# Reordering the first 18 microseconds of a mixer kernel: pair 8 before pair 6, tile 0 in halves, tile 3 through a DMA transpose

## The chip, the cores and the metric

The kernel runs on one core of one Trainium2 chip. The metric is the device time of one execution in microseconds. The time before the change is 136.75 us, the median of three runs (136.24, 136.75 and 136.87).

## The reference

The input x has 2048 rows of 512 values in bf16. A first layer normalizes each row, multiplies by w1 (512 x 512) and applies GELU. The result is shifted along the rows (one group of 128 columns by one row forward, one by one row back, one by two forward, one by two back), multiplied by w2 and added to x. A second layer normalizes that, multiplies by w3 (512 x 1792), applies GELU, multiplies by w4 (1792 x 512) and adds.

```python
def reference(x, w1, w2, w3, w4):
    B, S, D = x.shape
    h = _gelu(_layernorm(x, axis=-1) @ w1)
    c = D // 4
    g0 = jnp.pad(h[:, :, 0*c:1*c], ((0, 0), (1, 0), (0, 0)))[:, :S, :]
    g1 = jnp.pad(h[:, :, 1*c:2*c], ((0, 0), (0, 1), (0, 0)))[:, 1:, :]
    g2 = jnp.pad(h[:, :, 2*c:3*c], ((0, 0), (2, 0), (0, 0)))[:, :S, :]
    g3 = jnp.pad(h[:, :, 3*c:   ], ((0, 0), (0, 2), (0, 0)))[:, 2:, :]
    hs = jnp.concatenate([g0, g1, g2, g3], axis=-1) @ w2
    x1 = x + hs
    h2 = _gelu(_layernorm(x1, axis=-1) @ w3) @ w4
    return x1 + h2
```

## The kernel before

The 2048 rows are 16 tiles of 128 rows. Tile t holds the rows whose number modulo 16 is t, so a shift by one row is, for most tiles, the neighbouring tile.

The program is a list of named operations, each with what it reads and writes. `emit` turns these into semaphore waits. On each engine the operations run in order; the lists in `firsts` give that order by name for the start of the program, and what is not listed follows in the order of its `add`. An operation that waits holds up everything behind it on its engine. SyncE ("sp") is the queue from which nearly all DMAs are issued, so a DMA that waits for data holds up the DMAs listed behind it.

The first layer treats the tiles in two ways.

- Tiles 0 to 5 are "raw". The tile x is transposed as it was loaded: `tp` on TensorE (line 323) with `ev`, the copy out of PSUM on ScalarE (line 332), for tiles 0 to 3; `tdx`, a DMA transpose straight from memory (line 351), for tiles 4 and 5. `m1r` (line 378) multiplies it by w1 in four steps of 512 columns, `rc` (line 388) copies the result out, `zr` on VectorE (line 393) subtracts the mean times w1's column sums, and `g1r` (line 399) applies the scale and GELU. The column sums come from `cs0`, `cs1`, `cs2` and `cs` on TensorE (line 366), and `cse` copies them out (line 370). `th` is a DMA transpose of the result.
- Tiles 6 to 15 are normalized first: `st` and `ag` (statistics and aggregation on VectorE, lines 289 and 294), `rs` (the root, on GpSimd, for a pair of tiles, line 300), `nm` (the normalization on VectorE, line 309). A pair of them is then transposed, either by `tp` and `ev` (pairs 8 and 10) or by `td0`, a DMA transpose (line 343; pairs 6, 12 and 14). `m1p` multiplies a pair by w1 (line 410, 16 matmuls of 256 columns), and `g1p` or `g1s` applies GELU (lines 420 and 425).

`m2` (lines 436 and 450) multiplies by w2; a name with a, b or nothing at its end is a part of one tile's product. `x1` (line 460) adds x. The second layer repeats the statistics for x1 (`st1`, `ag1`, `rs1`, `nm1`) and transposes pairs by `td1` (line 343). `m3h` (line 492) multiplies the first four tiles, 8 to 11, by w3 in two halves: first the pair 8, which `td1_8` brings, then the pair 10 (`td1_10`). `m3` (line 468) and `m4` (line 511) do the rest, and `fin` and `out` add and store.

Loads: `ldx` for x (line 272), `ldw1` (line 542), `ldw2` (line 546), `ldw3a` (line 551, the first 1024 columns of w3, in four chunks), `ldw3b` (line 556), `ldw4`. Two of w1's chunks and x1 are loaded from ScalarE's queue. `wu` (line 534) is a run of matmuls on constants ahead of the first data.

PSUM has 8 banks. Raw tiles' transposes use banks 6 and 7, products of raw tiles banks 0 to 3, the column sums bank 4, the warm-up bank 5; the pair products use banks 2-3, 4-5, 0-1, 2-3 and 6-7.

Of the kernel before, what the change touches and what calls it, by code (L numbers as in the profile page):

```python
# [5 lines left out]
P = 128  # L6
ACT_F = mybir.ActivationFunctionType
ALU = mybir.AluOpType
BF16 = mybir.dt.bfloat16
# [17 lines left out]
class Program:  # L27
# [7 lines left out]
    def add(self, eng, name, fn, reads=(), writes=(), dma=False):  # L35
        self.ops.append(Op(name, eng, fn, reads, writes, dma))
# [135 lines left out]
def bass_standalone__mixer_s_mlp__prompt_kernel(nc: bass.Bass, x, w1, w2, w3, w4, out):  # L172
# [4 lines left out]
    DC = D // P  # L177
# [5 lines left out]
    xd = x[0].rearrange("(p t) d -> p t d", t=NT)  # L183
# [4 lines left out]
    with ExitStack() as es:  # L188
        sb = lambda name, shape, dt: es.enter_context(nc.sbuf_tensor(name, shape, dt))
        x_sb = sb("x_sb", [P, NT, D], BF16)  # L190
# [3 lines left out]
        xnT = sb("xnT", [P, NT, DC, P], BF16)  # L194
# [8 lines left out]
        w2_sb = sb("w2_sb", [P, DC, D], BF16)  # L203
        w3_sb = sb("w3_sb", [P, DC, F], BF16)
        w4_sb = sb("w4_sb", [P, FC, D], BF16)
        ident = sb("ident", [P, P], BF16)
# [3 lines left out]
        neghalf = sb("neghalf", [P, 4], F32)  # L210
        warm = sb("warm", [P, 1], F32)
        o_sb = sb("o_sb", [P, 4, D], BF16)
        ps = es.enter_context(nc.psum_tensor("ps", [P, 8 * 512], F32))
        psb = ps[:, :].bitcast(BF16)
        ones = nc.const_aps.tensor(1.0, [P, P], BF16)
        ones_wide = nc.const_aps.tensor(1.0, [P, 512], BF16)
        one_f = nc.const_aps.tensor(1.0, [P, 1], F32)

        hT = hTf[:, 16 : 16 + NT * DC * HW].rearrange("p (t j w) -> p t j w", t=NT, j=DC)
# [22 lines left out]
        W1 = [(("w1", c), 0) for c in range(DC)]  # L242
        W2 = [(("w2", c), 0) for c in range(DC)]
        pr = Program()
        add = pr.add

        def bank(b, n=1):
            return ps[:, 512 * b : 512 * (b + n)]

        def bres(b, n, tag):  # L250
            return [(("ps", b + i), tag) for i in range(n)]
# [19 lines left out]
        def load_x(t, n, eng="sp"):  # L271
            add(eng, f"ldx{t}", lambda e: e.dma_start(x_sb[:, t : t + n, :], xd[:, t : t + n, :]),  # L272
                writes=[(("x", i), 0) for i in range(t, t + n)], dma=True)
# [9 lines left out]
        def dst_of(layer, t):  # L283
            return (xn, t, ("xn", t), 0) if layer == 0 else (x1n, POS[t] % 8, ("x1n", POS[t] % 8), t)
# [29 lines left out]
        def tp(t, n, b, raw):  # L314
            src = x_sb if raw else xn
            rd = [(("x", i), 0) if raw else (("xn", i), 0) for i in range(t, t + n)]

            def f(e):
                ins = None
                for i in range(n):  # L320
                    for c in range(DC):
                        o = 1024 * b + (i * DC + c) * P
                        ins = e.transpose(psb[:, o : o + P], src[:, t + i, P * c : P * (c + 1)], ident[:])  # L323
                return ins

            add("pe", f"tp{t}", f, reads=rd + [("ident", 1)], writes=bres(b, 1, f"tp{t}"))

        def ev(t, n, b, eng="act"):
            src = psb[:, 1024 * b : 1024 * b + n * D]
            dst = xnT[:, t : t + n, :, :].rearrange("p t c s -> p (t c s)")  # L330
            if eng == "act":
                f = lambda e: e.activation(dst, src, ACT_F.Copy)  # L332
            else:
                f = lambda e: e.tensor_copy(dst, src)
            add(eng, f"ev{t}", f, reads=bres(b, 1, f"tp{t}"), writes=[(("xT", i), 0) for i in range(t, t + n)])


        def tdma(layer, t, n):
            dst = xnT if layer == 0 else x1nT
            src, k = dst_of(layer, t)[:2]  # L340
            p0 = t if layer == 0 else POS[t]
            add("sp", f"td{layer}_{t}",
                lambda e: e.dma_start(dst[:, p0 : p0 + n, :, :].rearrange("p t c s -> p (t c) s"),
                                      src[:, k : k + n, :].rearrange("p t d -> p (t d)"), transpose=True),
                reads=[dst_of(layer, i)[2:] for i in range(t, t + n)],
                writes=[(("xT", i) if layer == 0 else ("x1T", i), 0) for i in range(t, t + n)], dma=True)


        def tdma_x(t):
            add("sp", f"tdx_{t}",  # L350
                lambda e: e.dma_start(xnT[:, t : t + 2, :, :].rearrange("p t c s -> p (t c) s"),  # L351
                                      xd[:, t : t + 2, :].rearrange("p t d -> p (t d)"), transpose=True),
                writes=[(("xT", i), 0) for i in (t, t + 1)], dma=True)

        def tdma_h(t, n):
            add("sp", f"th_{t}",
# [17 lines left out]
        def m1r(t, b, c0=0, c1=DC):  # L374
            def f(e):
                ins = None
                for c in range(c0, c1):
                    ins = e.matmul(bank(b), xnT[:, t, c, :], w1_sb[:, c, :], start=(c == 0), stop=(c == DC - 1))  # L378
                return ins

            rd = [(("xT", t), 0)] + W1[c0:c1]
            if c0:
                rd += bres(b, 1, f"m1r{t}{c0}")
            end = f"{c1}" if c1 < DC else ""
            add("pe", f"m1r{t}{end}", f, reads=rd, writes=bres(b, 1, f"m1r{t}{end}"))

        def rc(t, b):
            add("act", f"rc{t}", lambda e: e.activation(yraw[:, t, :], bank(b), ACT_F.Copy),
                reads=bres(b, 1, f"m1r{t}"), writes=[(("yraw", t), 0)])
# [140 lines left out]
        def warmup(name, n, b):  # L530
            def f(e):
                ins = None
                for _ in range(n):
                    ins = e.matmul(bank(b), ones, ones_wide, start=True, stop=True)
                return ins

            add("pe", name, f, writes=bres(b, 1, name))
# [5 lines left out]
                writes=[(("w1", c), 0)], dma=True)  # L543

        def load_w2(c):
            add("sp", f"ldw2{c}", lambda e: e.dma_start(w2_sb[:, c, :], w2[P * c : P * (c + 1), :]),
                writes=[(("w2", c), 0)], dma=True)

        def load_w3a(c):
            add("sp", f"ldw3a{c}",  # L550
# [11 lines left out]
        load_w1(2, "act")  # L562
        load_w1(3, "sp")
        load_x(1, 1, "act")
        for t, n in ((6, 1), (7, 1), (2, 1), (8, 1), (3, 1), (9, 1), (10, 1), (11, 1), (12, 1), (13, 1), (14, 2), (4, 2)):
            load_x(t, n)
        for c in range(DC):
            load_w2(c)
        for c in range(DC):
            load_w3a(c)  # L570
        load_w3b()

        warmup("wu", 7, 5)
        YB = (0, 1, 2, 3, 0, 1)
        for c in range(DC):
            colsum(4, c)
        colsum_out(4)
        for t in range(R):
            if t < 4:
                tp(t, 1, 6 + t % 2, True)  # L580
                ev(t, 1, 6 + t % 2, "act")
            elif t == 4:
                tdma_x(t)
            cuts = [0, 1, 2, 3, 4] if t == 0 else [0, 2, 4] if t == 1 else [0, 4]
            for c0, c1 in zip(cuts, cuts[1:]):
                m1r(t, YB[t], c0, c1)
            rc(t, YB[t])
# [7 lines left out]
        for t in range(R, NT, 2):  # L595
# [2 lines left out]
                ev(t, 2, 6 + t // 2 % 2)  # L598
            else:
                tdma(0, t, 2)  # L600
        for t, b in ((6, 2), (8, 4), (10, 0), (12, 2), (14, 6)):
            m1p(t, b)
            if t == 10:
                g1s(t, b, 0)
                g1s(t, b, 1)
            else:
                g1p(t, b)
# [19 lines left out]
        for t in (8, 10):  # L627
# [7 lines left out]
            tdma(1, t, 2)  # L635

        firsts = {}
        firsts["pe"] = """wu tp0 cs0 cs1 m1r01 m1r02 tp1 m1r03 cs2 m1r0 cs tp2 m1r12 m1r1 tp3 m1r2 m1r3 m1r4 m1r5 tp8 m1p6
            tp10 m1p8 m1p10 m2_8a m2_9a m2_8 m2_9b m2_9 m2_10a m2_11a m2_12a m2_13a m1p12 m1p14 m2_10 m2_11
            m2_12b m2_13b m2_14a m2_15a m2_12 m2_13 m2_14b m2_15b m2_14 m2_15""".split()  # L640
        firsts["act"] = """ldw10 ldw12 ldx1 table ev0 ev1 rc0 ev2 ev3 rc1 rc2 rc3 rc4 rc5 ev8 cse g1p6 ev10 g1p8 g1s10 g1s11
            g1r0 g1r1 g1p12 g1p14 g2h_0_0_0 g2h_0_0_4 g1r2 g1r3 g2h_0_0_8 g2h_0_0_12 g1r4 g1r5""".split()
        firsts["dve"] = """pada padb padc padd pade padf st0_0 st0_6 st0_7 ag0_6 ag0_7
            st0_8 nm0_6 nm0_7 st0_9 ag0_8 ag0_9 st0_10 st0_11 nm0_8 nm0_9 ag0_10 ag0_11
            st0_12 nm0_10 nm0_11 st0_13 ag0_12 ag0_13 st0_14 st0_15 ag0_14 ag0_15 nm0_12 nm0_13 st0_1 ag0_0 ag0_1
            nm0_14 nm0_15 zr0 zr1 x1_8 x1_9 st1_8 st1_9 ag1_8 ag1_9 st0_2 nm1_8 nm1_9 st0_3 ag0_2 ag0_3 x1_10 x1_11 st1_10
            st1_11 ag1_10 ag1_11 x1_12 nm1_10 nm1_11 x1_13 x1_14 x1_15 zr2 zr3 st0_4 st0_5 ag0_4 ag0_5 zr4 zr5
            st1_12 st1_13 ag1_12 ag1_13""".split()
        firsts["pool"] = """ident0 ident1 neghalf stz ste rs0_6 rs0_8 rs0_10
            rs0_12 rs0_14 rs0_0 rs1_8 rs0_2 rs1_10""".split()  # L650
        firsts["sp"] = """ldx0 ldw11 ldx6 ldw13 ldx7 ldx2 ldx8 ldx3 ldx9 tdx_4 ldx10 ldx11 ldx12 td0_6 ldx13 ldx14 ldw20 ldw21 ldw22 ldw23 td0_12 td0_14 ldw3a0 ldw3a1
            ldw3a2 ldw3a3 th_0 td1_8 ldw3b ldx4 td1_10 th_2 th_4 td1_12 td1_14 ldw4""".split()

        slots = [4, 0, 2]
# [25 lines left out]
        def nm2(t):  # L680
            def f():
                norm(1, t)
                norm(1, t + 1)
                tdma(1, t, 2)

            return f
# [23 lines left out]
        for i, t in enumerate((0, 1, 2, 3, 4, 5, 6, 7)):  # L710
            b = (6, 7, 1)[i % 3]
# [11 lines left out]
        for q in (2, 3):  # L723
            for i in range(4):
                b = 6 + i % 2
# [40 lines left out]
```

## Time and profile before

| | |
|---|---|
| median of three runs | 136.75 us (136.24 to 136.87) |
| the profiled execution | 136.32 us |
| its span, first to last instruction | 134.5 us |
| TensorE busy | 130.8 us, 719 matmul records |
| VectorE busy | 58.3 us |
| ScalarE busy | 46.8 us |
| GpSimd busy | 12.5 us |
| DMA | 12.96 MB in 24376 packets |

The profiled execution is 1.8 us longer than its span; that part lies around the instructions. All times in the text below are counted from the start of the span. In the timeline and the chain the first number of a line is the start and the second the length. A matmul's record is longer than the distance to the next one, since matmuls are pipelined; the distances between starts tell how fast they go. Some matmul records are missing from the trace.

In the table of stretches, each engine has its busy time and, in brackets, its instructions; the last three numbers are the granted TensorE clock, the mean busy share of the DMA engines, and GB/s.

### The profile page before, as it was taken

The numbers are of one execution on the slowest core, as the hardware profiler recorded it, in microseconds if no ns is written. First come the engines' busy times: TensorE is split into PE (matmuls) and PEld (weight loads), VectorE is DVE, ScalarE is ACT, GpSimd is POOL, SyncE is SP. The second block draws the span as 40 slices with busy tenths as digits, with TensorE's granted clock in tenths as the row PEclk, the third lists the DMA queues.
The fourth block names the chain that finished last, engine by engine and source line by source line (L and its number), as shares of the span: only waits on it lengthen the run. The fifth ranks groups of instructions, "written<-read, shape, count | busy, mean of one in ns | idle before, by whom it ended". The sixth has DMA issues, their size and how long they took to land.

```text
span 134.5 us, 1794 instructions
## 1 busy us (share of the span) xinstructions
PE 130.8 (97%) x719; PEld 69.6 (52%) x729; DVE 58.3 (43%) x135; ACT 46.8 (35%) x56; POOL 12.5 (9%) x25
## 2 busy tenths in 40 slices
PE   7999999999999999999999999999999999999993
PEld 2446857678884444444444444444444444444452
DVE  0689999799967777762222000122200002322222
ACT  3488871507962036550001555200066630000000
POOL 2042422220330012220000000000000000000000
PEclk9999999999999999999999999999999999999999
DMA  4999379984465984444121000011110001111121
GB/s 123 317 247 217 115 145 246 255 292 83 78 128 100 295 262 78 78 80 78 39 68 49 5 0 0 0 39 39 41 37 5 0 0 39 39 39 39 44 75 42
DMA packets 24376, 12.96 MB, mean 96 GB/s; under 512 B 16688, under 2 KB 23600, under 8 KB 24368
## 3 DMA queue, kind: packets, MB, share of 16 engines
q1 hardware_dynamic: 23792, 12.42, 36.5%
q10 hardware_dynamic: 576, 0.43, 1.0%
q8 instruction: 6, 0.10, 0.3%
q14 instruction: 2, 0.02, 0.1%
HBM read 6.82 MB, written 2.10 MB: 66 GB/s over the span
## 4 chain that ended last, share of the span: by engine, by line
PE 89%; SPq 4%; DMA 2%; DVE 2%; issue 1%
PE ps L511 36%; PE ps L468 27%; PE ps L492 9%; PE ps L410 7%; PE ps L436 5%; PE ps L450 5%; DMA x_sb<-in_x_dram 2%; SPq L272 2%; SPq L351 1%; DVE st L289 1%; PE ps L323 1%; SPq L542 1%; DVE xn L309 0%; DVE o_sb L523 0%
## 5 line engine op out<-in xcount | busy, mean ns | idle before, releaser
L511 PE MATMUL ps<-w_sb,h2T 128*128 128x512 bf16 (+2 forms) x232 | 48.1, 366 | 0.3
L523 DVE TENSOR_TENSOR o_sb<-ps,x_sb 128x512 bf16<-128x512 f32 (+2 forms) x17 | 11.2, 660 | 61.2 <-PE ps L511 61.2
L479 ACT ACTIVATE h2T<-ps 128x1024 bf16<-128x1024 f32 x21 | 21.5, 1023 | 46.2 <-PE ps L468 46.2
L468 PE MATMUL ps<-x1nT,w_sb 128*128 128x512 bf16 x168 | 36.7, 379 | 0.0
L511 PEld LDWEIGHTS ps<-w_sb,h2T 128*128 128x128 bf16 x238 | 22.8, 98 | 25.9
L468 PEld LDWEIGHTS ps<-x1nT,w_sb 128*128 128x128 bf16 x168 | 16.4, 98 | 19.8
L289 DVE BATCH_NORM_STATS2 st<-x_sb 128x6 f32<-128x512 bf16 x32 | 20.9, 682 | 4.1 <-DMA x_sb<-in_x_dram 4.0
L300 POOL TENSOR_TENSOR rstd<-mv,neghalf 128x2 f32<-128x2 f32 x16 | 11.6, 725 | 46.1 <-DVE mv L294 46.1
L492 PE MATMUL ps<-x1nT,w_sb 128*128 128x256 bf16 x112 | 12.4, 273 | 0.0
L492 PEld LDWEIGHTS ps<-x1nT,w_sb 128*128 128x128 bf16 x112 | 11.0, 98 | 1.5
L460 DVE TENSOR_TENSOR x_sb<-ps,x_sb 128x512 bf16<-128x512 f32 x16 | 10.6, 685 | 2.5 <-PE ps L436 1.5
L410 PE MATMUL ps<-xnT,w_sb 128*128 128x256 bf16 x80 | 9.2, 273 | 0.0
L503 ACT ACTIVATE h2T<-ps 128x1024 bf16<-128x1024 f32 (+1 forms) x8 | 7.1, 913 | 6.0 <-PE ps L492 6.0
L410 PEld LDWEIGHTS ps<-xnT,w_sb 128*128 128x128 bf16 x80 | 7.6, 98 | 1.2
L309 DVE TENSOR_SCALAR x1n<-x_sb,mv,rstd 128x512 bf16<-128x512 bf16 x16 | 5.9, 409 | 5.3 <-POOL rstd L300 5.3
L450 PE MATMUL ps<-w_sb,hTf 128*128 128x512 bf16 x30 | 7.0, 379 | 0.1
L436 PE MATMUL ps<-w_sb,hTf 128*128 128x512 bf16 x31 | 6.9, 379 | 0.1
L378 PE MATMUL ps<-w_sb,xnT 128*128 128x512 bf16 x23 | 6.0, 382 | 0.1
L420 ACT ACTIVATE hTf<-ps 128x1024 bf16<-128x1024 f32 x4 | 4.1, 1023 | 4.2 <-PE ps L410 4.2
L332 ACT ACTIVATE xnT<-ps 128x512 bf16<-128x512 bf16 (+1 forms) x6 | 4.4, 738 | 2.3 <-PE ps L323 2.2
L436 PEld LDWEIGHTS ps<-w_sb,hTf 128*128 128x128 bf16 x32 | 3.1, 98 | 3.6
L294 DVE BATCH_NORM_AGGREGATE mv<-st 128x2 f32<-128x9 f32 x32 | 5.0, 185 | 0.0
(28 smaller groups left out, 36.8 us busy)
## 6 DMA issues: line engine op xcount, KB each, us to landing
out_dram<-o_sb SPq DMA_DIRECT2D x15, 128.0 KB, 1.8
w_sb<-in_w_dram SPq DMA_DIRECT2D x1, 1792.0 KB, 7.7
x_sb<-in_x_dram SPq DMA_DIRECT2D x11, 128.0 KB, 3.3
w_sb<-in_w_dram SPq DMA_DIRECT2D x4, 256.0 KB, 4.2
w_sb<-in_w_dram SPq DMA_DIRECT2D x6, 128.0 KB, 3.5
w_sb<-in_w_dram SPq DMA_DIRECT2D x1, 768.0 KB, 4.8
x_sb<-in_x_dram SPq DMA_DIRECT2D x2, 256.0 KB, 4.4
w_sb<-in_w_dram ACTq DMA_DIRECT2D x2, 128.0 KB, 3.2
```

The costliest lines, as they stand in the source:

```text
L289: add("dve", f"st{layer}_{t}", lambda e: e.bn_stats(st9[:, i, 0:6], src[:, t, :]), reads=[(r, 0)], writes=[(("st6", i), 0)])
L300: lambda e: e.tensor_tensor(rstd[:, i : i + n], mv[:, i : i + n, 1], neghalf[:, 0:n], ALU.pow),
L410: ins = e.matmul(dst, w1_sb[:, c, P * fc : P * (fc + 1)], xnT[:, t : t + 2, c, :], start=(c == 0), stop=(c == DC - 1))
L436: ins = e.matmul(bank(b), hTf[:, c0 : c0 + P], w2_sb[:, j, :], start=(j == 0), stop=(j == DC - 1))
L450: ins = e.matmul(bank(b), hTf[:, w[0] : w[0] + P], w2_sb[:, j, :], start=first and n == 0, stop=last and n == len(js) - 1)
L460: lambda e: e.tensor_tensor(x1_sb[:, t, :], bank(b), x_sb[:, t, :], ALU.add),
L468: ins = e.matmul(bank(b), w3_sb[:, c, P * fc : P * (fc + 1)], x1nT[:, 4 * q : 4 * q + 4, c, :], start=(c == 0), stop=(c == DC - 1))
L479: lambda e: e.activation(h2T[:, fc : fc + 2, q % 2, :], src, ACT_F.Gelu_apprx_tanh),
L492: ins = e.matmul(dst, w3_sb[:, c, P * (fc + i) : P * (fc + i + 1)], x1nT[:, t : t + 2, c, :], start=(c == 0), stop=(c == DC - 1))
L503: lambda e: e.activation(h2T[:, fc : fc + n, q % 2, 256 * k : 256 * (k + 1)], src, ACT_F.Gelu_apprx_tanh),
L511: ins = e.matmul(ps[:, 512 * b : 512 * b + c1 - c0], h2T[:, fc, q % 2, P * i : P * (i + 1)], w4_sb[:, fc, c0:c1], start=(fc == 0), stop=(f ...
L523: lambda e: e.tensor_tensor(o_sb[:, k % 4, c0:c1], ps[:, 512 * b : 512 * b + c1 - c0], x1_sb[:, t, c0:c1], ALU.add),
```

## The change

- The order on TensorE: tile 0's four matmuls go ahead of tile 1's transposes, three of the four column sums go later, tp8 goes ahead of m1r4, and pair 8 is multiplied ahead of pair 6 (the two swap their PSUM banks).
- Tile 0 is transposed and copied in two halves, into banks 6 and 7, and the first two matmuls read the first half.
- Tile 3 is transposed by a DMA of its own, `tdx_3`, in place of tp3 and ev3. x3 itself is loaded later, behind td0_14.
- The w1 chunk 3 goes ahead of x8 and x2; x8 and x9 are loaded ahead of x6 and x7.
- x12 and x13 are loaded by one DMA, and w2 by two in place of four.
- The warm-up has 14 matmuls of 256 columns in place of 7 of 512.
- VectorE, GpSimd and ScalarE follow: statistics of 8 and 9 ahead of 6 and 7, nm0_12 and nm0_13 ahead of st0_15, g1p8 ahead of g1p6, cse later.

```diff
+        def tp_part(t, c0, c1, b, part, res):
+            o = 1024 * b
+            n = (c1 - c0) * P
+
+            def f(e):
+                ins = None
+                for c in range(c0, c1):
+                    k = o + (c - c0) * P
+                    ins = e.transpose(psb[:, k : k + P], x_sb[:, t, P * c : P * (c + 1)], ident[:])
+                return ins
+
+            add("pe", f"tp{t}{part}", f, reads=[(("x", t), 0), ("ident", 1)], writes=bres(b, 1, f"tp{t}{part}"))
+            add("act", f"ev{t}{part}",
+                lambda e: e.activation(xnT[:, t, c0:c1, :].rearrange("p c s -> p (c s)"), psb[:, o : o + n], ACT_F.Copy),
+                reads=bres(b, 1, f"tp{t}{part}"), writes=[(res, 0)])
...
-        def tdma_x(t):
+        def tdma_x(t, n):
             add("sp", f"tdx_{t}",
-                lambda e: e.dma_start(xnT[:, t : t + 2, :, :].rearrange("p t c s -> p (t c) s"),
-                                      xd[:, t : t + 2, :].rearrange("p t d -> p (t d)"), transpose=True),
-                writes=[(("xT", i), 0) for i in (t, t + 1)], dma=True)
+                lambda e: e.dma_start(xnT[:, t : t + n, :, :].rearrange("p t c s -> p (t c) s"),
+                                      xd[:, t : t + n, :].rearrange("p t d -> p (t d)"), transpose=True),
+                writes=[(("xT", i), 0) for i in range(t, t + n)], dma=True)
...
-            rd = [(("xT", t), 0)] + W1[c0:c1]
+            rd = [(("xTa", t) if t == 0 and c1 <= 2 else ("xT", t), 0)] + W1[c0:c1]
...
-                    ins = e.matmul(bank(b), ones, ones_wide, start=True, stop=True)
+                    ins = e.matmul(ps[:, 512 * b : 512 * b + 256], ones, ones_wide, start=True, stop=True)
...
-        for t, n in ((6, 1), (7, 1), (2, 1), (8, 1), (3, 1), (9, 1), (10, 1), (11, 1), (12, 1), (13, 1), (14, 2), (4, 2)):
+        for t, n in ((8, 1), (6, 1), (7, 1), (2, 1), (3, 1), (9, 1), (10, 1), (11, 1), (12, 2), (14, 2), (4, 2)):
             load_x(t, n)
-        for c in range(DC):
+        for c in range(0, DC, 2):
             load_w2(c)
...
-        warmup("wu", 7, 5)
+        warmup("wu", 14, 5)
...
-            if t < 4:
+            if t == 0:
+                tp_part(0, 0, 2, 6, "a", ("xTa", 0))
+                tp_part(0, 2, 4, 7, "b", ("xT", 0))
+            elif t < 3:
                 tp(t, 1, 6 + t % 2, True)
                 ev(t, 1, 6 + t % 2, "act")
-            elif t == 4:
-                tdma_x(t)
+            elif t < 5:
+                tdma_x(t, 1 if t == 3 else 2)
...
-        for t, b in ((6, 2), (8, 4), (10, 0), (12, 2), (14, 6)):
+        for t, b in ((6, 4), (8, 2), (10, 0), (12, 2), (14, 6)):
...
-        firsts["pe"] = """wu tp0 cs0 cs1 m1r01 m1r02 tp1 m1r03 cs2 m1r0 cs tp2 m1r12 m1r1 tp3 m1r2 m1r3 m1r4 m1r5 tp8 m1p6
-            tp10 m1p8 m1p10 m2_8a m2_9a m2_8 m2_9b m2_9 m2_10a m2_11a m2_12a m2_13a m1p12 m1p14 m2_10 m2_11
+        firsts["pe"] = """wu tp0a tp0b cs0 m1r01 m1r02 m1r03 m1r0 tp1 cs1 cs2 tp2 m1r12 m1r1 m1r2 cs m1r3 tp8 m1r4 m1r5
+            m1p8 tp10 m1p6 m1p10 m2_8a m2_9a m2_8 m2_9b m2_9 m2_10a m2_11a m2_12a m2_13a m1p12 m1p14 m2_10 m2_11
             m2_12b m2_13b m2_14a m2_15a m2_12 m2_13 m2_14b m2_15b m2_14 m2_15""".split()
-        firsts["act"] = """ldw10 ldw12 ldx1 table ev0 ev1 rc0 ev2 ev3 rc1 rc2 rc3 rc4 rc5 ev8 cse g1p6 ev10 g1p8 g1s10 g1s11
+        firsts["act"] = """ldw10 ldw12 ldx1 table ev0a ev0b ev1 ev2 rc0 rc1 rc2 rc3 ev8 rc4 rc5 cse ev10 g1p8 g1p6 g1s10 g1s11
             g1r0 g1r1 g1p12 g1p14 g2h_0_0_0 g2h_0_0_4 g1r2 g1r3 g2h_0_0_8 g2h_0_0_12 g1r4 g1r5""".split()
-        firsts["dve"] = """pada padb padc padd pade padf st0_0 st0_6 st0_7 ag0_6 ag0_7
-            st0_8 nm0_6 nm0_7 st0_9 ag0_8 ag0_9 st0_10 st0_11 nm0_8 nm0_9 ag0_10 ag0_11
-            st0_12 nm0_10 nm0_11 st0_13 ag0_12 ag0_13 st0_14 st0_15 ag0_14 ag0_15 nm0_12 nm0_13 st0_1 ag0_0 ag0_1
+        firsts["dve"] = """pada padb padc padd pade padf st0_0 st0_8 ag0_8 st0_9 ag0_9
+            st0_6 st0_7 ag0_6 ag0_7 nm0_8 nm0_9 nm0_6 nm0_7 st0_10 st0_11 ag0_10 ag0_11
+            st0_12 nm0_10 nm0_11 st0_13 ag0_12 ag0_13 st0_14 nm0_12 nm0_13 st0_15 ag0_14 ag0_15 st0_1 ag0_0 ag0_1
...
-        firsts["pool"] = """ident0 ident1 neghalf stz ste rs0_6 rs0_8 rs0_10
+        firsts["pool"] = """ident0 ident1 neghalf stz ste rs0_8 rs0_6 rs0_10
...
-        firsts["sp"] = """ldx0 ldw11 ldx6 ldw13 ldx7 ldx2 ldx8 ldx3 ldx9 tdx_4 ldx10 ldx11 ldx12 td0_6 ldx13 ldx14 ldw20 ldw21 ldw22 ldw23 td0_12 td0_14 ldw3a0 ldw3a1
+        firsts["sp"] = """ldx0 ldw11 ldw13 ldx8 ldx2 ldx9 ldx6 ldx7 tdx_3 tdx_4 ldx10 ldx11 ldx12 td0_6 ldx14 ldw20 ldw22 td0_12 td0_14 ldx3 ldw3a0 ldw3a1
             ldw3a2 ldw3a3 th_0 td1_8 ldw3b ldx4 td1_10 th_2 th_4 td1_12 td1_14 ldw4""".split()
```

More of the change, by code (lines that the diff above doesn't have):

```diff
@@ L215, in bass_standalone__mixer_s_mlp__prompt_kernel @@
         ones = nc.const_aps.tensor(1.0, [P, P], BF16)
-        ones_wide = nc.const_aps.tensor(1.0, [P, 512], BF16)
+        ones_wide = nc.const_aps.tensor(1.0, [P, 256], BF16)
         one_f = nc.const_aps.tensor(1.0, [P, 1], F32)
@@ L545, in load_w2 @@
         def load_w2(c):
-            add("sp", f"ldw2{c}", lambda e: e.dma_start(w2_sb[:, c, :], w2[P * c : P * (c + 1), :]),
-                writes=[(("w2", c), 0)], dma=True)
+            add("sp", f"ldw2{c}",
+                lambda e: e.dma_start(w2_sb[:, c : c + 2, :],
+                                      w2[P * c : P * (c + 2), :].rearrange("(c p) f -> p c f", p=P)),
+                writes=[(("w2", c + i), 0) for i in range(2)], dma=True)
         def load_w3a(c):
```

## The prediction

> **What bounds the kernel now.** I read the page first, then the chain that ended last, then TensorE's timeline, then SyncE's queue with the landings.
>
> The page's busy times:
>
> ```profile
> PE 130.8 (97%) x719; PEld 69.6 (52%) x729; DVE 58.3 (43%) x135; ACT 46.8 (35%) x56; POOL 12.5 (9%) x25
> ```
>
> TensorE is the bound, so the question is where its other 3% lies. The chain (start, length):
>
> ```profile
> 9.68 1.29 DVE st L289 x2
> 10.97 0.64 DVE xn L309 x2
> 11.61 0.05 issue
> 11.66 0.62 PE ps L323 x8
> ...
> 25.47 2.97 PE ps L450 x13
> 28.44 12.23 PE ps L492 x112
> ```
>
> From 11.66 us the chain is TensorE without a break, but for 0.05 us pieces, until 132.22. Before 11.66 it ran through VectorE and the loads. Only the first 11.7 us can give time back; anything after can only lose some. TensorE's timeline there:
>
> ```profile
> 0.77 3.14 PE L534 MATMUL ps<-const-bfloat16-1.0 128*128 128x512 bf16 x7 [0.77 <-PEq L751]
> 3.71 0.63 PE L323 MATMUL ps<-ident,x_sb 128*128 128x128 bf16 x4
> 4.14 1.06 PE L366 MATMUL ps<-w_sb,const-bfloat16-1.0 128*128 128x512 bf16 x2
> 7.70 0.39 PE L323 MATMUL ps<-ident,x_sb 128*128 128x128 bf16 x4
> 7.93 3.62 PE L378 MATMUL ps<-w_sb,xnT 128*128 128x512 bf16 x15
> 11.66 0.62 PE L323 MATMUL ps<-ident,xn 128*128 128x128 bf16 x8
> 12.16 1.92 PE L410 MATMUL ps<-xnT,w_sb 128*128 128x256 bf16 x16
> ```
>
> Starts follow each other every 0.427 us at 512 columns until 5.19 us (clock still half) and every 0.216 us after; 0.109 at 256 columns, 0.056 for a transpose. By that pitch the 7.93 group (16 matmuls; one record is missing) is over at 11.38, so tp8 waited 0.28 for xn9. m1p6 waited 0.05 for td0_6, landed at 12.12. With 0.04 before m1r01 and slips of 0.01, all idle time after the warm-up is 0.40 us.
>
> SyncE's queue (start, issue time), then the landing after the issue start for three of its DMAs: x13 (9.69), x14-15 (10.31) and td1_8 (23.65):
>
> ```profile
> 4.97 1.40 SPq L351 DMA_TRANSPOSE xnT<-in_x_dram  x1
> 9.69 1.06 SPq L272 DMA_DIRECT2D x_sb<-in_x_dram  x2
> 16.43 2.68 SPq L343 DMA_TRANSPOSE xnT<-xn  x2
> 19.15 2.01 SPq L551 DMA_DIRECT2D w_sb<-in_w_dram  x4
> 23.65 1.32 SPq L343 DMA_TRANSPOSE x1nT<-x1n  x1
> ```
>
> ```profile
> x_sb<-in_x_dram SPq DMA_DIRECT2D x1, 128.0 KB, 2.8
> ...
> x_sb<-in_x_dram SPq DMA_DIRECT2D x1, 256.0 KB, 3.9
> ...
> x1nT<-x1n SPq DMA_TRANSPOSE x1, 3.5
> ```
>
> td1_8 lands at 27.15; TensorE wants it at 28.27 (first m3h). That slack of 1.1 us is what I watch, because the DMA engines have none there (DMA share, second from the end):
>
> ```profile
> 18.00:28.20 10.20, 10.10 (x63) 6.17 (x63) 8.98 (x21) 4.35 (x6) 1.62 (x4) 1.00 1.04 241
> ```
>
> **The change part by part.**
>
> *Warm-up of 14 halves*: the same 3584 columns, so 3.71 us again. Zero, bounds ±0.05 (the first matmul's pitch was 0.38, not 0.43).
>
> *Tile 0 in halves.* A 512-column copy took 0.60 us, a 1024-column one 1.02; that is 0.17 + 0.43 per 512, so 0.38 for a half. ev0a starts 0.04 after its transposes' record ends, at 4.17, and ends at 4.55. m1r01 follows at 4.61 instead of 5.03, behind one column sum (cs0, till 4.57) instead of two. TensorE only swaps work; its idle 0.04 stays. w1's last chunk, now third on SyncE, lands when x6 did (4.95) and is needed at 5.53. Then m1r03, m1r0 (till 5.75), tp1 (5.97), cs1, cs2, tp2 (6.63). tp1 is behind tile 0's matmuls now, so ev1 runs 6.17 to 6.77 and m1r12 starts at 6.82: a new wait of 0.20. Covered up to here.
>
> *Tile 3 by DMA* removes tp3: 4 × 0.056 = 0.22 of TensorE, and ev3 of ScalarE. m1r2, cs end at 8.77 and m1r3 wants tdx_3. No single-tile DMA transpose is in the trace. Its issue lies between a plain one (0.43) and the pair's 1.40; I take half the pair, 0.70. tdx_3 then issues at 4.49 and tdx_4 at 5.24. Landing goes by the engines, which are full: x8, fourth now, lands at 5.50 as ldw13 did; four loads of 0.38 follow; the pair's packets then needed about 1.9 (9.28 less x9's end), the single one, behind no plain load of its own, 0.6 more. That is 8.3 for tdx_3 (wanted 8.71) and 9.5 for tdx_4 (bounds 9.3 and 10.2; wanted 10.02). No wait, up to 0.2 in the range.
>
> *Pair 8 first.* x9, sixth, lands at 6.49; st0_9, ag0_9 end at 7.43; POOL's root takes 0.70 plus 0.12 of handing over, till 8.22, while VectorE does tiles 6 and 7 until 8.8; nm0_8, nm0_9 end at 9.53. tp8 stands behind m1r3 (9.63) and waits no more: 0.28 saved. m1r4, m1r5 (till 11.80) hide ev8 (10.33 to 11.35). m1p8 ends 13.55; tp10 wants xn11, which ends about 13.45. m1p6, now 14.00, wants td0_6: nm0_7 ends at 10.44 (it waits for the second root), issue 10.47, plus 3.2 is 13.7. m1p10 ends 17.49 against 17.87.
>
> So at m1p10 TensorE is ahead by 0.22 (tp3) + 0.40 (old idle) − 0.24 (new idle) = 0.38 us.
>
> *Loads merged.* x12 now comes with x13: one issue fewer, but x12 alone had been wanted at 11.80 and 256 KB issued at 7.8 lands at 11.7 by the 3.9 of x14. That could put tp10 0.05 late. The Trainium skill (DMA: Bandwidth & Descriptors, Rules for kernel authors) says to coalesce small transfers into one large one; by that rule this term would be zero or a gain, where the row makes it 0 to 0.05. The w2 pairs, issued by 13.3, are wanted at 17.49 and 4.4 after an issue at 12.84 is 17.24: nothing.
>
> *What td0_6's later issue pushes back.* This is the term that counts. td0_6 holds SyncE from wherever nm0_7 ends: 10.47 instead of 8.41. Behind it stand x14-15, w2, td0_12, td0_14. x14 issues at 11.74 instead of 10.31. Bounds 2.8 and 3.9; I take 3.9 less 0.4, since x13 no longer goes ahead of it: 15.25 (14.55 to 15.65). VectorE wanted it at 14.2, and it is queued in order: st0_14 15.27, nm0_12/13 at 15.87 and 16.20 (pitches 0.60 and 0.33), st0_15 16.52, ag0_15 till 17.44, root till 18.28, nm0_15 till 19.05. td0_12 (16.6 + 3.2 = 19.8, wanted 20.9) is in time. td0_14 issues at 19.08 instead of 17.88; alone a pair lands 3.1 later, 22.2 (wanted 22.65).
>
> *x3 moved behind td0_14.* One more 128 KB and 0.58 of SyncE ahead of w3a. Engines at a share of 1.04 pass a delay on: td1_8 lands later by 1.15 (td0_14) and 0.38 (x3), less some 0.2, as the engines were not quite full at 21 to 23 us: 27.15 + 1.33 = 28.48. Its own issue (24.4 + 3.1 = 27.5) is not the limit. TensorE wants it at 28.27 − 0.38 = 27.89, a landing by 27.84. Stall 0.64.
>
> Sum: −0.38 + 0.64 = +0.26 us. Behind it w3b (31.1, wanted 32.0) and td1_10 (34.1, wanted 34.5) are just in time. On the profiled execution's 136.32 this gives 136.58; the median of the runs, 136.75, stands 0.43 above it, so 137.0.
>
> **The rivals.**
>
> *A: the gain arrives.* If x14 takes the 2.8 of x13, td0_14 issues at 18.4, and if x3 fits into the DMA gaps, td1_8 lands near 27.8. Then −0.38: 136.37. For it: engines 88 to 95% busy after the transposes. Against: w3a took 4.0 to 4.5 to land, so the queue was backed up.
>
> *B: slower.* td1_8 is later still. It decides from a landing of 28.9 (stall 1.06, net +0.68). With x14 at 15.65 and x3 paid in full it lands at 29.0 to 29.2, net +0.8 to +1.0: 137.55 to 137.75. For it: x14's own row is 3.9, and td1_10's 4.5 shows that a transpose can land far behind its issue.
>
> *C: an early wait comes back.* tdx_4 pays for two changes from plain loads to transposes instead of one and lands after 10.02; the 0.2 to 0.3 won at tp8 is lost at m1r4. td1_8's stall shrinks by as much, so the end is the same, 137.0; without that stall 136.6.
>
> *D: the clock rises at another time.* The pitch halved at 5.19 us; every 0.5 us earlier or later moves the end by 0.25, and the runs already differ by 0.63. The Trainium skill (TensorE: Matmul & The Clock Gate, Part 1) has a free-running window of about 3.4 us, so the rise may move by half a microsecond from run to run; by that 136.75 or 137.25.
>
> *E: the order holds but saves nothing*, because tp8 still waits: xn9 would have to end 2 us later than worked out. I see no row for it.
>
> **How the numbers follow.** Forecast 0.45, A 0.25, B 0.17, C 0.08, D 0.05. Low end: A, less 0.2 of run spread, 136.2. High end: B's 137.75. The forecast's own range, for x14 between its bounds, is 136.6 to 137.4. About 0.5% (0.68 us) is what a measurement of this kernel can tell from no change. Faster by that much needs A and an early clock: 0.05. Slower: B and the forecast's upper edge, 0.20. The rest, 0.75, is no change.
>
> **What would show it.** Right: no tp3; tp8 within 0.1 us of m1r3; m1p8 from 11.8; a gap of about 0.2 before m1r12; m1p10's end near 17.5; st0_14 waiting for its load till about 15.2; td0_14 issued near 19.1; a gap at the first m3h with td1_8 landing near 28.5. Wrong: m3h starting at 27.9 with no gap (A), a gap over 1 us (B), or a gap at m1r3, m1r4 or m1p6.

## The result, and the profile after

The changed kernel takes 137.51 us (median of 15 runs, 136.88 to 138.23) against 136.44 us before (15 runs, 136.24 to 136.87): a ratio of 1.0072, 95% interval 1.0058 to 1.0087. It is slower by more than the 0.5% that counts as measurable here. The profiled execution took 137.06 us, 0.74 more than the one of before; its span is 135.2 us. The runs also spread twice as far as before.

The page's busy times after the change:

```profile
PE 131.7 (97%) x732; PEld 70.1 (52%) x732; DVE 58.1 (43%) x135; ACT 46.3 (34%) x56; POOL 12.5 (9%) x25
```

TensorE is still the bound by share, and the share doesn't tell what happened. The chain that ended last does (start, length):

```profile
2.13 3.99 DMA x_sb<-in_x_dram
...
12.18 3.30 DMA x_sb<-in_x_dram
15.50 0.69 DVE st L289
...
24.82 4.02 DMA x1nT<-x1n
28.85 0.14 issue
28.98 12.39 PE ps L509 x112
```

Before, TensorE carried the chain alone from 11.66 us on. Now it takes over only at 28.98. The chain until then is the forecast's: x8 into VectorE, td0_6 into the load of x14-15 (12.18), VectorE, and td1_8, which lands at 28.85. (The eighteen lines between 15.50 and 24.82 are VectorE's steps, a root on GpSimd and short issues.)

TensorE's timeline, at the places where it waits:

```profile
6.65 0.40 PE L323 MATMUL ps<-ident,x_sb 128*128 128x128 bf16 x4
8.88 1.03 PE L395 MATMUL ps<-w_sb,xnT 128*128 128x512 bf16 x4
9.92 0.62 PE L323 MATMUL ps<-ident,xn 128*128 128x128 bf16 x8
28.02 0.82 PE L467 MATMUL ps<-w_sb,hTf 128*128 128x512 bf16 x3 [0.25 <-DMA hTf<-hraw]
28.98 1.25 PE L509 MATMUL ps<-x1nT,w_sb 128*128 128x256 bf16 x10
```

By the pitch of 0.216, tp2 (6.65) waited 0.13 for x2, tp8 (9.92) 0.17 for xn9, the matmul at 28.02 waited 0.41 for th_0, and the first m3h 0.30 for td1_8. No tp3 is left. m1p8 starts at 12.11 and m1p10 ends at 17.84, where it ended at 17.87 before: the start gained 0.03 us, and the two late waits cost 0.71. From the first m3h to the end of the span 106.25 us pass after the change and 106.23 before, so the whole difference has arisen by then.

SyncE's queue (start, issue time):

```profile
4.50 2.62 SPq L368 DMA_TRANSPOSE xnT<-in_x_dram  x2
10.89 1.24 SPq L360 DMA_TRANSPOSE xnT<-xn  x1
12.18 0.58 SPq L272 DMA_DIRECT2D x_sb<-in_x_dram  x1
16.86 3.61 SPq L360 DMA_TRANSPOSE xnT<-xn  x2
24.82 1.99 SPq L360 DMA_TRANSPOSE x1nT<-x1n  x1
```

tdx_3 and tdx_4 take 2.62 us together, where 0.70 and 1.40 had been forecast. td0_6 goes at 10.89, x14-15 at 12.18. The second transpose of the 16.86 line, td0_14, goes at 19.24, against 17.88 before.

### The profile page after: what moved, and what is told of

The parts are those of the page before. It is cut to its first block, busy times and chain, and to the rows that moved or that the text cites. A ratio compares the mean times of both kernels' runs of the same rounds, so it can differ in the third digit from the quotient of the medians.

```text
span 135.2 us, 1808 instructions
## 1 busy us (share of the span) xinstructions
PE 131.7 (97%) x732; PEld 70.1 (52%) x732; DVE 58.1 (43%) x135; ACT 46.3 (34%) x56; POOL 12.5 (9%) x25
## 4 chain that ended last, share of the span: by engine, by line
PE 77%; DVE 10%; DMA 8%; POOL 1%; SPq 1%; issue 1%
PE ps L528 36%; PE ps L485 27%; PE ps L509 9%; DMA x_sb<-in_x_dram 5%; PE ps L453 5%; DVE st L289 5%; DMA x1nT<-x1n 3%; DVE xn L309 1%; POOL rstd L300 1%; DVE mv L294 1%; DVE zraw L410 1%; DVE x_sb L477 1%; SPq L559 1%; DVE x1n L309 1%; SPq L272 0%
## 5 line engine op out<-in xcount | busy, mean ns | idle before, releaser
L528 PE MATMUL ps<-w_sb,h2T 128*128 128x512 bf16 (+2 forms) x238 | 48.9, 367 | 0.0
L467 PE MATMUL ps<-w_sb,hTf 128*128 128x512 bf16 x32 | 7.4, 380 | 0.2 <-DMA hTf<-hraw 0.2
L453 PE MATMUL ps<-w_sb,hTf 128*128 128x512 bf16 x32 | 7.1, 379 | 0.0
L467 PEld LDWEIGHTS ps<-w_sb,hTf 128*128 128x128 bf16 x32 | 3.0, 98 | 3.9 <-DMA hTf<-hraw 0.7
L453 PEld LDWEIGHTS ps<-w_sb,hTf 128*128 128x128 bf16 x32 | 3.1, 98 | 3.6
```

The costliest lines, as they stand in the source:

```text
L453: ins = e.matmul(bank(b), hTf[:, c0 : c0 + P], w2_sb[:, j, :], start=(j == 0), stop=(j == DC - 1))
L467: ins = e.matmul(bank(b), hTf[:, w[0] : w[0] + P], w2_sb[:, j, :], start=first and n == 0, stop=last and n == len(js) - 1)
L528: ins = e.matmul(ps[:, 512 * b : 512 * b + c1 - c0], h2T[:, fc, q % 2, P * i : P * (i + 1)], w4_sb[:, fc, c0:c1], start=(fc == 0), stop=(f ...
```

## The experiments

Two theories stood against each other. Q: SyncE's queue passes td0_6's later issue on, through x14 and VectorE to td0_14, and x3, moved behind td0_14, adds to it; so th_0 and td1_8 come late. S: the start itself costs the time, and the late waits only follow. Each kernel was run beside the kernel before; ratios are to that.

**x14_ahead.** From the changed kernel:

```diff
-ldx12 td0_6 ldx14 ldw20 ldw22 td0_12 td0_14 ldx3
+ldx12 ldx14 td0_6 ldw20 ldw22 td0_12 td0_14 ldx3
```

> After, with the load of x14-15 issued ahead of td0_6 instead of behind it. Theory Q (SyncE's queue): td0_6's later issue held x14 back, x14 held VectorE, and so td0_14, w3a, th_0 and td1_8 came late and TensorE waited 0.41 us for th_0 and 0.30 us for td1_8. Then x14 lands near 13, td0_14 issues near 18.4 instead of 19.24, both waits shrink by 0.6 to 0.8 in all, and the time is 136.7 to 137.0; td0_6 may land 0.3 later and make m1p6 wait up to 0.2. Rival S (the start): the time was lost in the first 12 us (a later clock, tp8's wait) and the late waits only follow; then no change, 137.2 to 137.8.

137.22 us, ratio 1.0052 (1.0036 to 1.0069): some 0.3 less than the change, if anything, and far from the 0.7 of Q. x14 did land at 13.39 and no longer held VectorE. With x3 still behind td0_14 both late waits stayed (0.47 and 0.34). In this trace x12 also landed at 12.73 instead of 11.64, so tp10 waited 0.53; the order alone doesn't explain that, since in the four other kernels with x14 right behind x12 it landed between 11.58 and 12.01.

**x3_ahead.**

```diff
-ldw20 ldw22 td0_12 td0_14 ldx3 ldw3a0
+ldw20 ldw22 ldx3 td0_12 td0_14 ldw3a0
```

> After, with x3 loaded behind the w2 loads and ahead of td0_12, where the DMA engines are idle, instead of behind td0_14. Q: x3 lands near 17.6, w3a issues 0.8 us earlier, th_0 and td1_8 land 0.4 to 0.8 earlier, the 0.71 us of late waits falls to 0.1 to 0.4: 137.0 to 137.2. S: no change, 137.2 to 137.8.

137.46 us, ratio 1.0068 (1.0048 to 1.0088): no change. x3 landed at 17.72 as meant, but x14 still held VectorE (15.96), td0_14 went at 19.72, and the late waits were 0.43 and 0.33.

**x14_x3_ahead.** Both edits together.

> After, with both loads moved: x14-15 ahead of td0_6 and x3 ahead of td0_12. Q: no late wait is left at th_0 and td1_8, and only the start's gain or loss remains: 136.3 to 136.7, level with before. S: 137.2 to 137.8, as after.

136.61 us, ratio 1.0008 (0.9997 to 1.002): level with before. One late wait of 0.12 is left in the trace. So the two delays don't add up: in the changed kernel undoing one gives 0.3 us or nothing, and undoing both gives 0.9. That is why each single edit looked idle.

**tile3_alone.** The kernel before, with this part of the change only:

```diff
-... m1r12 m1r1 tp3 m1r2 m1r3 ...      ev2 ev3 rc1
+... m1r12 m1r1 m1r2 m1r3 ...          ev2 rc1
-... ldx8 ldx3 ldx9 tdx_4 ...  td0_14 ldw3a0
+... ldx8 ldx9 tdx_3 tdx_4 ... td0_14 ldx3 ldw3a0
```

> Before, with one part of the change alone: tile 3 transposed by its own DMA, tp3 and ev3 gone, x3 loaded behind td0_14. Q: td1_8 had 1.1 us of slack, and x3 uses 0.4 to 0.8 of it; tp8 still waits for xn9 until 11.6, so the 0.22 us of removed transposes only lengthens that wait: 136.3 to 136.7, no change. S: if the additional DMA transpose is what costs at the start, m1r3 or m1r4 waits for it and the time is 136.8 or more.

136.96 us, ratio 1.0031 (1.002 to 1.0043): slower, which Q had not expected. td1_8 landed at 28.22, so I suspected that the late x3 had used up the slack.

**tile3_x3_early.** The same with x3 loaded ahead of td0_12.

> Before with tile 3 by DMA, as in tile3_alone, but x3 loaded ahead of td0_12. Theory Q': in tile3_alone td1_8 landed at 28.22, so the late x3 used up all of its 1.1 us of slack and costs 0.4 us in the median by itself; then here td1_8 lands 0.5 to 1.0 earlier and the time is 136.3 to 136.6, level with before. Rival S': the third DMA transpose at the start costs it; then 136.8 to 137.1, as tile3_alone.

136.93 us, ratio 1.0034 (1.0021 to 1.0046): the suspicion was wrong, x3's place is not it. This trace has a cause. SyncE's queue, then VectorE's timeline, then TensorE's:

```profile
4.50 2.62 SPq L351 DMA_TRANSPOSE xnT<-in_x_dram  x2
7.17 1.53 SPq L272 DMA_DIRECT2D x_sb<-in_x_dram  x3
```

```profile
10.38 1.29 DVE L289 BATCH_NORM_STATS2 st<-x_sb 128x6 f32<-128x512 bf16 x2 [0.94 <-DMA x_sb<-in_x_dram]
11.59 0.72 DVE L309 TENSOR_SCALAR xn<-x_sb,mv,rstd 128x512 bf16<-128x512 bf16 x2
```

```profile
12.36 0.62 PE L323 MATMUL ps<-ident,xn 128*128 128x128 bf16 x8 [0.77 <-DVE xn L309]
```

A transpose of one tile holds SyncE for 1.27 us, as one of two tiles does (1.23 to 1.40 for td0, td1 and tdx_4 in the trace of before). x10 is issued at 7.17 instead of 6.42 and lands at 10.36; in this order st0_10 stands ahead of nm0_8, so tp8 starts at 12.36 instead of 11.66. In the full change nm0_8 and nm0_9 stand ahead of st0_10, and this cost does not appear. For tile3_alone itself the cause is not shown: in its trace (136.67, its fastest run) x10 landed at 9.94 and tp8 did not wait, because TensorE was late for another reason. The matmul pitch halved only at 6.8 us there, against 5.19 before.

**warmup_7.** The changed kernel with the old warm-up of 7 matmuls of 512 columns.

> After, with the warm-up as before: 7 matmuls of 512 columns. If the halves are free, as worked out: the same as after, 137.2 to 137.8. Rival W: the 14 halves make the clock rise later; then the time falls by up to the 0.2 us that the rise was later in the trace, 136.9 to 137.2.

137.51 us, ratio 1.0072 (1.0046 to 1.0098): the same as the change, so the halves are free as far as this interval tells.

**w3a_ahead.** x14_x3_ahead, and:

```diff
-ldx3 td0_12 td0_14 ldw3a0 ldw3a1 ldw3a2
+ldx3 ldw3a0 ldw3a1 td0_12 td0_14 ldw3a2
```

> x14_x3_ahead, and half of w3a (512 KB) issued ahead of td0_12, into the idle stretch of the DMA engines. Q: td1_8, which still landed at 28.38 there, lands at 27.0 to 27.7; no late wait is left and what remains is the gain of the start: 136.1 to 136.5. S: the start gains nothing, 136.5 to 136.8.

136.57 us, ratio 1.0004 (0.9988 to 1.002). td1_8 lands at 27.46, and TensorE (its timeline) runs into m3h without a gap, 0.216 after the last m2 matmul:

```profile
25.05 3.62 PE L467 MATMUL ps<-w_sb,hTf 128*128 128x512 bf16 x15
28.50 2.67 PE L509 MATMUL ps<-x1nT,w_sb 128*128 128x256 bf16 x23
```

What is left lies at the start: by the pitch tp2 waited 0.43 for x2 and tp8 0.36 for xn9, and m1p10 ended at 18.10, 0.23 later than before.

With the late part mended the kernel is level with before, not 0.38 us ahead. Moving x14, x3 and half of w3a took back 0.94 of the change's 1.07 us, so the late waits carry nearly all of it. S is right in one thing: the start gains nothing that can be measured.

**w3a_x8_ahead.** w3a_ahead, with x8 loaded ahead of w1's last chunk:

```diff
-ldw11 ldw13 ldx8 ldx2
+ldw11 ldx8 ldw13 ldx2
```

> w3a_ahead, and x8 loaded ahead of w1's last chunk, which undoes that part of the change. Q: x8 lands 0.4 to 0.6 earlier, tp8 no longer waits (0.17 in after), the pair chain runs 0.4 earlier: 136.0 to 136.4. Against it, m1r0 may wait for w1 by 0.1 to 0.3: then as w3a_ahead. S: 136.5 to 136.8.

136.49 us, ratio 1.0009 (0.9991 to 1.0027). In the trace x8 landed at 5.16, tp8 did not wait, and m3h started at 28.23 against 28.27 before; the median shows no gain.

**x8_ahead.** The changed kernel with that last edit alone.

> After, with x8 loaded ahead of w1's last chunk and nothing else. Q: x8, which landed at 6.12 where 5.50 was forecast, lands at 5.1 to 5.3; statistics, nm0_7, td0_6, x14 and td0_14 move 0.3 to 0.6 earlier, and the late waits at th_0 and td1_8 shrink by as much: 136.9 to 137.2. If the late waits hang on x3 and w3a alone: 137.4 to 137.6, as after.

138.27 us, ratio 1.0118 (1.0089 to 1.0147): worse, where 136.9 to 137.2 was expected. x8 landed at 6.65. A load lands in sixteen parts in the trace; fifteen of x8's were there by 5.62. m1r0 then waited for w1 until 7.05.

**x8_ahead_again.** The same kernel, loaded anew.

> The same kernel as x8_ahead, loaded anew. There five of six runs lay at 138.23 to 138.48 and one at 137.18, and in the profiled one x8 landed at 6.66 instead of 5.2; w3a_x8_ahead has the same first nine loads, and there x8 landed at 5.16. If the late landing belongs to this order of loads: 138.2 to 138.5 again. If it belongs to the execution or to how the program was loaded: most runs at 136.9 to 137.4, x8 at 5.1 to 5.3, and Q's first expectation holds.

137.38 us, ratio 1.0065 (1.0039 to 1.0091), no different from the change. x8 landed at 5.70, 4.0 us after its issue, against 5.0 in the first trace; 5.1 to 5.3 had been hoped for.

So the 0.9 us between the two medians does not belong to the kernel. The two traces differ in how the early loads landed. Why is open: the second loading was also on another chip, and no run separates the two. The interval of one set of runs does not cover such a shift, so a single median of the changed order or its variants is less sure than its interval says. The kernel before stayed within 136.44 to 136.57 over five such sessions.

**x14_late_alone.** The kernel before, with x14-15 behind the w2 loads:

```diff
-ldx13 ldx14 ldw20 ldw21 ldw22 ldw23 td0_12
+ldx13 ldw20 ldw21 ldw22 ldw23 ldx14 td0_12
```

> Before, with the load of x14-15 issued behind the four w2 loads, so that it lands at 15.3 to 15.8 as in after; all else as before. Q: st0_14 waits 1.0 to 1.5 us, td0_14 issues near 18.9 and td1_8 lands near 28.0, just inside the 1.1 us of slack: 136.4 to 136.9; the delay costs little alone and much only together with the late x3 and an earlier TensorE. If it costs alone what after lost: 137.2 or more.

137.43 us, ratio 1.0066 (1.0044 to 1.0088). That is nearly as much as the whole change costs, and the slack did not hold it. VectorE's timeline, then TensorE's:

```profile
16.21 1.29 DVE L289 BATCH_NORM_STATS2 st<-x_sb 128x6 f32<-128x512 bf16 x2 [1.82 <-DMA x_sb<-in_x_dram]
```

```profile
22.35 3.67 PE L410 MATMUL ps<-xnT,w_sb 128*128 128x256 bf16 x32 [0.36 <-DMA xnT<-xn]
29.61 1.14 PE L492 MATMUL ps<-x1nT,w_sb 128*128 128x256 bf16 x9
```

VectorE stood 1.82 us for x14. In the order of before st0_15 also stands ahead of nm0_12, so td0_12 (landing 22.31) held m1p12 for 0.52, and td1_8, landing at 29.47, held m3h for 0.30. Together that is 0.82 of the 1.34 us by which m3h came later. The other 0.51 had arisen by m1p10's end, before x14 matters to TensorE: in this execution too the pitch halved only near 6.8 us.

**tp1_ahead.** w3a_x8_ahead, with tp1 ahead of m1r03 and m1r0.

> w3a_x8_ahead, with tile 1's transposes ahead of m1r03 and m1r0, so that ev1 ends before tp2 and m1r12 no longer waits its 0.20 us. Q: m3h starts 0.2 earlier, at 28.0, but td1_10, which landed at 34.27, is then wanted at 34.1: 136.2 to 136.5. S: no change against w3a_x8_ahead, 136.4 to 136.7.

136.66 us, ratio 1.0019 (1.0003 to 1.0034): no gain. In the profiled execution, the slowest of its twelve, x8 landed at 6.77 and x1 at 6.97, and tp1, now two matmuls earlier, waited for it. No version beats the kernel before.

## Why the prediction was right or wrong

The range of 136.2 to 137.75 held 137.51, and the mechanism named as the one that counts is the one that the chain and the experiments show. That the range held is partly luck. The forecast of +0.26 us was laid on 136.75, a median of three runs. Over 15 runs the kernel before takes 136.44, and from there the same sums give 136.7, with an upper end of 137.44. The change measured +1.07, four times the forecast and a little beyond B's +1.0. So 137.0 and "no change" at 0.75 were too kind: it came out on rival B's side, which had 0.17. In the profiled execution td1_8 landed at 28.85, 0.05 before B's deciding point.

- *Warm-up*: right, warmup_7.
- *Tile 0 in halves*: right. The half copies took 0.38, m1r01 started at 4.61.
- *The start's gain of 0.38* is mis-sized. It measured 0.03 at m1p10's end in the profile, and nothing in the median of w3a_ahead, whose interval leaves room for at most 0.16. The 0.35 missing there are: the halving of the pitch, which fell at 5.41 instead of 5.19 (0.11); tp8's wait (0.17), which had been put at nothing because x8 and x9 were taken to land at 5.50 and 6.49 and landed at 6.12 and 6.91; and about 0.07 of smaller waits, at tp10 (0.03) among them. Fourteen of x8's sixteen parts had landed by 5.60. x2, fifth on the queue, landed at 6.60 where the fifth load had landed at 5.87 before, and its wait at tp2 replaced most of the one forecast at m1r12.
- *Tile 3 by DMA*: half the pair's issue time was the wrong choice between two bounds; it is 1.27, near the upper one. In the change this moved the issues of x10 to x12 back by 0.7 us against before and was hidden there; alone it costs 0.4 us. The 1.9 us for the pair's packets is not the difference that the forecast names: x9 landed at 8.21 before, and 9.28 less that is 1.07. tdx_3 and tdx_4 landed at 8.70 and 9.68 (8.3 and 9.5), and nothing waited for them.
- *td0_6 and x14*: right. td0_6 went at 10.89 (10.47), x14 landed at 15.48 (15.25), td0_14 went at 19.24 (19.08).
- *td1_8* is the mis-sized term that decided the time: it landed at 28.85 instead of 28.48. w3a, ahead of it on SyncE, was issued 2.17 us later than before, 1.36 of it from td0_14 (1.15 in the sum) and 0.80 from the issue of x3 (0.38 in the sum, as transfer). *The first m3h*: 28.98 instead of 28.53. The stall of 0.64 measured 0.71, but 0.41 of it came earlier than foreseen, at the last m2 matmuls, which need th_0. th_0 stands ahead of td1_8 on the same engines; the forecast did not ask who waits for th_0.
- *Sum*: +0.26 forecast, +0.71 at m3h and +0.74 in the profiled time. Of the 0.45 between forecast and m3h, td1_8's landing is 0.37, and the step from there to the first matmul (0.13 instead of 0.05) the rest. The start's missing 0.35 is no part of it: TensorE is not in the chain before 28.98, and had it been ahead by 0.38, its stall would have been longer by as much. The stall's 0.71 comes near the forecast's 0.64 only because the two errors offset each other.
- *Adding the two delays* is not how they act. x14_ahead, x3_ahead and x14_late_alone keep late waits with one delay left, while tile3_alone, with x3 late and td0_14 at 18.00, has none in its trace. What makes them act so in the DMA queues is not shown: in x14_ahead w3a's first chunk was issued at 20.76 instead of 21.32 and landed at 25.35 instead of 24.59.
- *Rival A* fails: no such gain in any run. *C* did not occur in the change: m1r3 and m1r4 did not wait. *D*, the clock, is part of the start's missing gain, by 0.11 in this trace; how much it does to the median is not settled. That it is a clock is inferred from the pitch: the profile's granted clock reads 1.00 in these first microseconds too. *E* had the right outcome for the start, but tp8's wait, E's reason, is 0.17 of the 0.35.

What the medians hold beyond the profiled executions, 1.07 against 0.74, was not traced run by run. One trace shows where it can come from. warmup_7 differs from the changed kernel in the warm-up alone, and its profiled execution took 138.09 us. There x8 landed at 6.45, x14 at 16.02, td0_14 went at 19.78, and the same two late waits were larger: 1.14 for th_0, whose line on TensorE's timeline stands below, and 0.31 for td1_8.

```profile
29.05 0.82 PE L467 MATMUL ps<-w_sb,hTf 128*128 128x512 bf16 x3 [0.97 <-DMA hTf<-hraw]
```

In all fourteen traces 106.23 to 106.30 us pass from the first m3h to the end of the span.

## What to carry to other kernels

When TensorE has next to no idle time left, an edit at the start can be paid for by whatever it pushes back on the queues, so follow every DMA behind the one that moves until its consumer, and ask of each landing who else waits for it. Slack that can't be seen in the chain (here 1.1 us ahead of td1_8) is what absorbs late loads; once it is used up, the median pays. When one of two delays is undone and nothing happens, undo both before dropping the theory.

## What the runs showed of the hardware

- A DMA transpose of one tile (128 KB) occupied SyncE's queue for 1.27 us, one of two tiles 1.23 to 1.40 in the trace of before (th_0 alone 1.61): the issue time did not follow the size.
- The same early load, third on SyncE, landed 3.5, 4.0, 5.0 and 5.1 us after its issue in four traces with the same loads ahead of it (w3a_x8_ahead, x8_ahead_again, x8_ahead, tp1_ahead). In x8_ahead the first of its sixteen parts came at 4.12, the fifteenth at 5.62 and the last at 6.65.
- The moment at which the matmul pitch halves lay between 4.6 us (x14_x3_ahead) and 6.8 us (tile3_alone) after the start of the span, over kernels whose TensorE work is nearly the same until then. The Trainium skill (TensorE: Matmul & The Clock Gate, Part 1) explains a variable moment by a free-running window; its half microsecond either way is less than what these traces show.
